# A fused window attention and MLP kernel: the order of the first loads and casts, and the last layer 1 by seven block products

## The chip, the core and the metric

The kernel runs on one core of a Trainium2 chip. The metric is the device time of one execution in microseconds (us), as the median of several executions. Times inside an execution come from the hardware profiler, which records one execution; they are counted from the start of its span. The engines are named as in the profile: PE (TensorE, matrix products), PEld (its weight loads), DVE (VectorE), ACT (ScalarE), POOL (GpSimd) and SP (SyncE, which here only issues loads).

## The reference, cut to what matters

```python
# q, k, v: [8 batches, 8 heads, 576 rows, 64]
scores = (q @ k.T) / 8                       # per batch and head
mask = (rel >= 0) & (rel < 64)               # rel = row of q - row of k
attn = softmax(where(mask, scores, -1e9))
x = (attn @ v), heads side by side           # [8, 576, 512]
xn = (x - mean(x)) / sqrt(var(x) + 1e-6) * g_ln
out = x + relu(xn @ w_ch1) @ w_ch2           # w_ch1 512x2048, w_ch2 2048x512
```
All inputs and the output are fp32; the kernel casts its operands to fp16.

## The kernel before, in words

*Tiles.* Each row sees the 64 rows up to itself, so attention works on blocks of 128 rows: a block needs its own keys and values and the 64 before it. The MLP runs on groups of 512 rows. Groups g = 0 to 7 are the first 512 rows of batch g; the ninth, the tail group (g = 8, `NGRP - 1`, in the code `last`), gathers the last 64 rows of all eight batches. A group has four blocks, called kb or j.

*Attention of one block.* q and k are loaded in halves (`load_qk`, L76), cast to fp16 (`cast_q`, L149) and, for the first three batches, transposed on PE (`t_main`, L268, evicted by `evac`, L262); later batches are transposed by DMA (`x_main`). `load_v` (L161) and `cast_v` (L178) bring v into `vA`; `vB` holds v shifted by 64 rows, made in batch 0 and partly in batch 1 by casts straight from the fp32 load (`vB_cur`, `vB_prev`, L194 and L197). `s_mm` (L302) computes the scores, exponentials on ACT follow, `s_mask` (L355) applies the mask on DVE; in batch 0 PE adds a mask bias instead (`pe_mask`). `b_step` (L369) multiplies by v, divides by the row sum and takes mean and variance; `r_step` (L397) computes the reciprocal deviation on ACT; `z_step` (L406) makes the normalized block z; `zt_step` (L447) transposes z on PE into `zT` and ACT copies it out.

*MLP of one group.* It is a list of small "units", built by `mlp_units` (L503). Layer 1 (`l1`, L508) makes 128 of the 2048 hidden columns for 512 rows in four matmuls of 512 columns, and ACT rectifies the result into `hrT`: 16 such units in groups 2 to 8. Group 0 does half of its layer 1 in halves of 256 rows (`l1_half`, L544), and group 1 all of it. Layer 2 of group 0 is `l2_three` (L557) and `l2` (L521), that of group 1 `l2`. From group 2 on layer 2 is done by `product` (L573): a 2x2 block product with seven block multiplications in place of eight (a Strassen form), each in two units of eight matmuls of 256 columns. It needs sums and differences of blocks of `hrT`, made by `presum` (L493) on DVE as eight additions of 128x1024, and of blocks of w2, made once by `t_weights` (L476). After each product `post` (L600) adds the PSUM bank to the output tile on DVE.

*What sets the order.* The kernel is under a manual schedule: each engine runs its instructions in the order of the program text. In the main loop (L762) every group's units are issued one after the other, and `at(i, f, ...)` hangs a step f behind unit i; so attention of batch g + 1 is interleaved with the MLP of group g by unit numbers written out by hand. `bz` (L769) hangs b_step, r_step and z_step at i, i + 1, i + 2. `pace` (L444) is a tiny POOL copy that makes POOL wait for its operand before the casts behind it.

*The head.* L647 to L654 issue the loads of batch 0 and of w1. w1 comes in eight tiles of 256x512, each cast (and scaled by g) in two parts by `w1_cast` (L232). L666 to L684 hold POOL's casts of batch 0, then memsets for batch 1; L694 to L724 the first scores and blocks, with dummy matmuls (`keep_clock`). Then SP gets batch 1's first half of q and k and the first four w2 loads of 512 KB (L727 to L729). The rest of the loads is issued inside `rest_of_loads` (L731), which hangs at unit 7 of group 0 and also holds POOL's casts in order:

```python
        cast_qk(1, 0)
        for i in range(8):
            w2_cast(i)
            if i < 4:
                w2_load(i + 4)
        load_v(1, 0, 2)
        ...
```
The w2 staging tiles are four buffers (pool `pwst`, tag `wld`), so the load of tile i + 4 comes after the cast of tile i. All loads above are on SP's queue, and their landings are counted by eight semaphores of the program, used in turn.

*The PSUM banks.* Pools `ps_s` (tag `sc`), `ps_x` (`xps`), `ps_t` (`tp`) and `ps_mm` (`mm`) have two buffers of a bank each, `ps_x` one of two banks. Layer 1 takes turns in `mm` and `tp`; `product` holds its X in `tp` and its Y and Z in `mm`. In the tail group no attention is left, so `sc` and `xps` are free.

Of the kernel before, what the change touches and what calls it, by code (L numbers as in the profile page):

```python
# [18 lines left out]
def kernel(  # L19
# [136 lines left out]

    def alloc_v(b):
        vA[b] = p_va.tile([128, 4, H, D + 1], FP16, tag="vA", name=f"vA_{b}")
        nc.gpsimd.memset(vA[b][:, :, :, D:D + 1], 1.0)
# [29 lines left out]
    def init_vB(b):  # L189
        alloc_vB(b)  # L190
        nc.gpsimd.memset(vB[b][:, :, :, D:D + 1], 1.0)
        nc.gpsimd.memset(vB[b][0:64, 0, :, D:D + 1], 0.0)

    def vB_cur(b, c, eng):  # L194
        evac(eng, vB[b][64:128, c, :, 0:D], v32[b][0:64, c])
# [66 lines left out]
    def evac(x, out, in_):  # L262
        if x == 0:
            nc.scalar.copy(out=out, in_=in_)
        else:
            nc.vector.tensor_copy(out=out, in_=in_)
# [235 lines left out]

    def mlp_units(g, split=0, two=False):  # L503
# [123 lines left out]
        if g == 1:  # L627
            return units
        for hc in range(split, NHC):
            units.append(lambda hc=hc: l1(hc))  # L630
# [36 lines left out]
    alloc_qkT(0)  # L667
    cast_q(0, 0, 0)
    alloc_v(0)
    cast_q(0, 1, 0)  # L670
    init_vB(0)
    cast_v(0, 0, 1)
# [3 lines left out]
    cast_v(0, 3, 4)  # L676
    w1_cast(0, 0, nc.gpsimd)
    w1_cast(1, 0, nc.gpsimd, 0, 256)
    w1_cast(1, 0, nc.gpsimd, 256, 512)
    for i, lo in ((2, 0), (3, 0), (2, 256)):  # L680
        w1_cast(i, 0, nc.gpsimd, lo, lo + 256)

    for f in (alloc_qkT, alloc_v, init_vB):
        f(1)  # L684
# [12 lines left out]
    t_main(0, 1, 0, 1)  # L697
    keep_clock(1, ps_mm, "mm")
    vB_cur(0, 0, 0)
    vB_cur(0, 1, 0)  # L700
    vB_prev(0, 0, 1)
    vB_prev(0, 1, 1)
# [13 lines left out]
    vB_cur(0, 3, 1)  # L716
    vB_prev(0, 2, 1)
    keep_clock(1)
    zt_step(0, 1)
    w1_cast(0, 1, nc.scalar)  # L720
# [7 lines left out]
    for i in range(4):  # L728
        w2_load(i)  # L729

    def rest_of_loads():  # L731
        cast_qk(1, 0)
        for i in range(8):
            w2_cast(i)
            if i < 4:
                w2_load(i + 4)
        load_v(1, 0, 2)
        cast_v(1, 0, 1)
        cast_v(1, 1, 2)
        load_qk(1, 1)  # L740
        load_v(1, 2, 4)
        cast_qk(1, 1)
        cast_v(1, 2, 3)
        cast_v(1, 3, 4)
        load_qk(2, 0)
        load_qk(2, 1)
# [15 lines left out]
    for g in range(NGRP):  # L762
# [33 lines left out]
        if g == 0:  # L796
# [29 lines left out]
            at(42, zt_step, 1, 1)  # L826
            at(43, t_main, 1, 0, 1, 0)
            at(44, load_v, 2, 0, 4)
# [10 lines left out]
        if g == 1:  # L839
# [27 lines left out]
            for j in range(4):  # L867
                at((13, 16, 19, 22)[j], s_mm, 2, j)
                at((14, 17, 20, 23)[j], s_mask, 2, j)
                bz((16, 19, 22, 25)[j], 2, j)  # L870
                at((20, 23, 26, 29)[j], zt_step, 2, j)
        if g > 0:
            if g == 1:
                for u, i, c in ((12, 1, 0), (13, 1, 1), (14, 2, 0), (15, 2, 1)):
                    at(u, t_weights, i, c)
            if g == 2:
                at(9, late_masks, 8)
                for u, i, c in ((2, 3, 0), (3, 3, 1), (8, 4, 0), (24, 4, 1)):
                    at(u, t_weights, i, c)
            for u, i, c in () if g == 1 else (  # L880
                    (5, 3, 0), (9, 3, 1), (13, 1, 0), (13, 2, 0), (16, 1, 1), (16, 2, 1), (20, 4, 0), (22, 4, 1)):
                at(u, presum, g, i, c)
# [22 lines left out]
        if 0 < g and b + 1 < B:  # L905
# [5 lines left out]
            if g == 1:  # L911
                at(10, alloc_qkT, n)
                for j, (x, half) in enumerate(((0, 0), (1, 0), (0, 1), (1, 1))):
                    u = (16, 19, 22, 27)[j]
                    at(u, (lambda: pace(zsd[(b, 3)][:, 0:1])) if j == 3 else lambda j=j: pace(rcps[(b, j)][:, 0:1]))
                    at(u, cast_q, n, x, half)
# [61 lines left out]
```

## Time and profile before

| what | value |
|---|---|
| three executions | 303.74, 303.81 and 304.11 us (median 303.81) |
| the profiled execution, as a whole | 304.84 us |
| its span in the profile | 303.0 us |
| mean granted PE clock | 0.993 |
| first scores of the first block start | 10.73 us |
| first use of the fifth w2 tile by PE | 42.82 us |
| layer 1 of the tail group | 271.74 to 285.56 us |
| layer 2 of the tail group | 285.56 to 297.80 us |
| HBM traffic | 36.70 MB read, 9.44 MB written |

A line of the profile's groups reads: source line, engine, operation, tile, count, then busy time, mean of one, and the idle time ahead of them with what ended it. A line of the chain of waits reads: start in us, length in us, engine and tile, source line. A row of the 40 slices shows the busy share in tenths, 7.6 us a digit. In a timeline the first two columns are start and length, and the bracket at the end holds the idle time ahead and what ended it.

### The profile page before, as it was taken

The page shows a single profiled execution, that of the slowest core. Times are in us where ns is not written, and L with a number is a line of the kernel's source. Part 1 is how long each engine was busy: PE and PEld are TensorE (multiplying, and loading weights), DVE is VectorE, ACT ScalarE, POOL GpSimd, SP SyncE. Part 2 cuts the span into 40 slices and gives each one's busy share as a digit, 9 for nine tenths or more (in the row PEclk, how much of TensorE's full clock was granted, in tenths as well). Part 3 has the DMA queues.
Part 4 walks back from the last instruction along what each step waited for, and adds up shares of the span by engine and source line. Part 5 has one row for each costly group of instructions (what it writes and reads, how often), then busy time and mean ns, then how long its engine had stood idle before and what let it go on. Part 6 is the DMA issues. An engine that isn't in the chain of part 4 may idle for free.

```text
span 303.0 us, 7956 instructions
## 1 busy us (share of the span) xinstructions
PE 289.7 (96%) x3259; PEld 187.1 (62%) x3259; DVE 194.8 (64%) x353; ACT 189.9 (63%) x372; POOL 108.8 (36%) x194
## 2 busy tenths in 40 slices
PE   5788999999999999999999999999999999999993
PEld 2456544765854478547855784578457845884582
DVE  0696317457984997389638954895489877641362
ACT  3598733576856894589368937892785978307500
POOL 3778775997786203400440043004171010000000
PEclk9799999999999999999999999999999999999999
DMA  6999799999957969997999899899967930003005
GB/s 186 279 368 386 252 272 276 278 303 279 219 115 209 259 127 168 298 247 128 189 319 228 105 200 322 196 118 204 276 123 153 158 141 0 2 21 117 2 0 138
DMA packets 108371, 58.03 MB, mean 192 GB/s; under 512 B 82240, under 2 KB 98112, under 8 KB 108336
## 3 DMA queue, kind: packets, MB, share of 16 engines
q1 hardware_dynamic: 103696, 45.50, 67.1%
q0 software_dynamic: 3680, 11.52, 12.6%
q10 hardware_dynamic: 960, 0.53, 0.6%
q8 instruction: 25, 0.41, 0.6%
q14 instruction: 10, 0.08, 0.1%
HBM read 36.70 MB, written 9.44 MB: 152 GB/s over the span
## 4 chain that ended last, share of the span: by engine, by line
PE 75%; DMA 11%; SPq 5%; POOL 3%; ACT 2%; DVE 2%; issue 1%; POOLq 0%
PE hps L512 33%; PE wX L590 16%; PE wZ L590 8%; PE wY L590 4%; DMA v<-in_v_dram 4%; PE xps L383 4%; SPq L83 3%; DMA w2s<-in_moe_w_ch_dram 3%; PE sc L326 2%; PE ch L525 2%; DMA vt<-vA 2%; SPq L173 2%; PE hph L549 2%; DMA qk<-in_k_dram 1%; PE ztp L453 1%; PE sc L333 1%
## 5 line engine op out<-in xcount | busy, mean ns | idle before, releaser
L512 PE MATMUL hps<-zT,w1g 128*128 128x512 f16 x480 | 109.7, 379 | 0.0
L516 ACT ACTIVATE hrT<-hps 128x512 f16<-128x512 f32 x120 | 71.3, 596 | 54.0 <-PE hps L512 52.8
L512 PEld LDWEIGHTS <-w1g 128*128 128x128 f16 x480 | 44.8, 98 | 49.5
L590 PEld LDWEIGHTS <-sw 128*128 128x128 f16 x448 | 43.5, 98 | 5.0
L590 PEld LDWEIGHTS <-hrT 128*128 128x128 f16 x336 | 32.4, 98 | 5.4
L367 DVE TENSOR_TENSOR pt<-pt,mask 128x1024 f16<-128x1024 f16 x28 | 20.0, 713 | 20.9 <-ACT pt L347 12.6
L207 POOL DMA_DIRECT2D vB<-vA x10 | 5.1, 518 | 77.9 <-ACT vA L145 77.6
L472 POOL DMA_DIRECT2D out_dram<-osb x20 | 13.2, 660 | 54.4 <-DVE osb L608 50.1
L392 DVE BATCH_NORM_STATS2 stats<-xn 128x6 f32<-128x512 f32 x36 | 25.0, 695 | 1.2
L390 DVE TENSOR_TENSOR xn<-xps,rcp 128x512 f32<-128x512 f32 x36 | 24.9, 691 | 1.2
L347 ACT ACTIVATE pt<-sc 128x512 f16<-128x512 f32 x40 | 23.7, 594 | 2.5 <-PE sc L326 2.5
L501 DVE TENSOR_TENSOR sw<-hrT 128x1024 f16<-128x1024 f16 x28 | 19.0, 678 | 9.7 <-ACT hrT L516 9.7
L549 PE MATMUL hph<-zT,w1g 128*128 128x256 f16 x192 | 23.7, 273 | 0.4 <-POOL w1g L240 0.2
L414 DVE TENSOR_SCALAR z<-xn,mv,rs 128x512 f16<-128x512 f32 x32 | 19.8, 617 | 5.0 <-ACT rs L404 4.5
L608 DVE TENSOR_TENSOR osb<-wX,xn 128x512 f32<-128x512 f32 (+1 forms) x24 | 14.9, 621 | 9.9 <-PE wX L590 9.9
L353 ACT ACTIVATE pt<-sc 128x512 f16<-128x512 f32 x32 | 17.6, 594 | 5.0 <-PE sc L333 4.6
L147 POOL CAST qk<-qk 128x1024 f16<-128x1024 f32 x16 | 17.1, 1076 | 9.0 <-DMA qk<-in_q_dram 6.0
L549 PEld LDWEIGHTS <-w1g 128*128 128x128 f16 x192 | 17.9, 98 | 3.5 <-POOL w1g L240 0.5
L383 PEld LDWEIGHTS <-pt 128*64 128x64 f16 x576 | 12.1, 110 | 12.8 <-issue 8.5
L525 PE MATMUL ch<-w2s,hrT 128*128 128x512 f16 x80 | 19.8, 379 | 0.0
L456 ACT COPY zT<-ztp 128x512 f16<-128x512 f16 x21 | 12.3, 584 | 9.6 <-PE ztp L453 9.5
L554 ACT ACTIVATE hrT<-hph 128x512 f16<-128x512 f32 x24 | 14.2, 598 | 3.4 <-PE hph L549 3.2
(108 smaller groups left out, 439.3 us busy)
## 6 DMA issues: line engine op xcount, KB each, us to landing
w2s<-in_moe_w_ch_dram SPq DMA_DIRECT2D x12, 512.0 KB, 9.4
out_dram<-osb POOLq DMA_DIRECT2D x12, 512.0 KB, 7.0
qk<-in_q_dram SPq DMA_DIRECT2D x10, 512.0 KB, 7.7
qk<-in_k_dram SPq DMA_DIRECT2D x10, 512.0 KB, 9.5
v<-in_v_dram SPq DMA_DIRECT2D x40, 128.0 KB, 5.9
qk<-in_q_dram SPq DMA_DIRECT2D x12, 256.0 KB, 5.0
qk<-in_k_dram SPq DMA_DIRECT2D x12, 256.0 KB, 4.8
v<-in_v_dram SPq DMA_DIRECT2D x12, 256.0 KB, 5.7
```

Source lines behind the costliest of these rows:

```text
L347: nc.scalar.activation(out=pt[:, par].rearrange("k h w (p j) -> k (h w) p j", j=4), in_=sc[:, :].rearrange("k h w (j p) -> k (h w) p j", j=4),
L367: nc.vector.tensor_tensor(out=ptv, in0=ptv, in1=mb, op=ALU.mult)
L383: nc.tensor.matmul(out=xps[64 * r:64 * r + 64, h, :D + 1], lhsT=pt[:, par, hp, r, :], rhs=rhs, start=True, stop=True)
L390: nc.vector.tensor_tensor(out=xn, in0=xps[:, :, 0:D], in1=rcp_b, op=ALU.mult)
L392: nc.vector.bn_stats(out=stats, in_=xn.rearrange("p h d -> p (h d)"))
L414: nc.vector.tensor_scalar(out=z, in0=x, scalar1=mv[:, 0:1], scalar2=rss[(g, kb)][:, 0:1], op0=ALU.subtract, op1=ALU.mult)
L501: nc.vector.tensor_tensor(out=S[i], in0=a, in1=b, op=op)
L512: nc.tensor.matmul(out=hps, lhsT=w1g[:, kc, 128 * hc:128 * (hc + 1)], rhs=zT[g][:, kc, :], start=(kc == KCS[0]), stop=(kc == KCS[-1]),)
L516: nc.scalar.activation(out=hrT[:, hc, :], in_=hps, func=AF.Relu, bias=0.0, scale=1.0)
L525: nc.tensor.matmul(out=ch[kb], lhsT=hrT[:, hc, 128 * kb:128 * (kb + 1)], rhs=w2s[:, hc, :], start=(hc == 0), stop=(hc == NHC - 1),)
L549: nc.tensor.matmul(out=hps[:, e], lhsT=w1g[:, kc, 128 * hc:128 * (hc + 1)], rhs=zT[g][:, kc, 256 * half:256 * half + 256], start=(kc == KC ...
L590: nc.tensor.matmul(out=xyz[bank][t * two_banks][:, t], lhsT=lhsT, rhs=rhs, start=bool(first and (t == 0 or two_banks) and hc == 0), stop=( ...
```

## The change

1. *First casts.* The cast of the first half of k of batch 0 goes from POOL to DVE, in two instructions (`cast_k0`), and the eviction of its transposition from DVE to ACT. Of the vB casts of batch 0, those of blocks 0 and 1 all go to DVE, two of the later ones to POOL (a new case `x == 2` in `evac`). Two w1 casts go to DVE. The memsets of batch 1 (`alloc_qkT`, `alloc_v`, `init_vB`) move ahead of the first casts on POOL.
2. *Loads of batch 1.* v and the second half of q and k of batch 1 are issued behind the first four w2 loads, ahead of w2 loads five to eight. In `rest_of_loads` their casts move between the w2 casts, and the loads of q and k of batch 2 forward to the places of the casts.
3. *Slots in group 0.* `t_main(1, 0, 1, 0)` comes before `zt_step(1, 1)`; the load of v of batch 2 is issued four units earlier.
4. *Slots in group 1.* Some b_step, zt_step and cast slots of batch 2 and 3 move one unit later.
5. *The tail group's layer 1.* It is done by seven block multiplications in place of eight: `l1_seven` has 28 units of four matmuls of 256 columns in place of 16 units of four matmuls of 512. Sums of w1 blocks (`l1_wsum`, eight DVE instructions of 128x1024) and of zT blocks (`l1_zsum`, four of 128x512) are made in group 7, in buffers of the q and k loads. Results of n = 2, 5, 6 are copied by ACT into held tiles, that of n = 4 is rectified by ACT, those of n = 1, 7, 3 are added to a held one and then rectified, two DVE instructions each. The presums of layer 2 hang at later units of the tail group, and its first product is inserted among the last units of layer 1.

```diff
+    def cast_k0():
+        t = qk32.pop((0, 1, 0))
...
+        for e in range(2):
+            nc.vector.tensor_copy(out=dst[:, :, e], in_=t[:, 512 * e:512 * e + 512].rearrange("p (j d) -> p j d", d=D))
...
+        elif x == 2:
+            nc.gpsimd.tensor_copy(out=out, in_=in_)
...
+    def l1_wsum(i, c):
+        A = [[w1g[:, 2 * kb + c, 1024 * d:1024 * d + 1024] for kb in range(2)] for d in range(2)]
+        if c == 0:
+            s1w[i] = p_in.tile([128, 2, 1024], FP16, tag=f"qk32_{i % 2}", name=f"s1w_{i}")
...
+        nc.vector.tensor_tensor(out=S[i], in0=a, in1=b, op=op)
...
+    def l1_zsum(g, i):
+        if i % 2:
+            s1z[i // 2] = p_in.tile([128, 2, 2, 256], FP16, tag=f"qk16_{i // 2}", name=f"s1z_{i}")
...
+        nc.vector.tensor_tensor(out=T[i], in0=z_block(g, *a), in1=b, op=ALU.subtract)
...
+    def l1_seven(g, hrT):
...
+        def product(r, n):
...
+                    nc.tensor.matmul(out=ps[:, e], lhsT=lhsT, rhs=rhs, start=bool(first and e == 0 and c == 0),
+                                     stop=(e == 1 and c == 1), skip_group_check=True)
...
+            if n in (2, 5, 6):
+                held[(r, n)] = p_pt.tile([128, 2, 256], FP32, tag="pt", name=f"l1h_{r}_{n}")
+                nc.scalar.copy(out=held[(r, n)], in_=ps)
+            elif n == 4:
+                nc.scalar.activation(out=hrT[:, down, lo], in_=ps, func=AF.Relu, bias=0.0, scale=1.0)
+            else:
+                out, other = {1: (hrT[:, up, lo], 2), 7: (hrT[:, down, hi], 5), 3: (hrT[:, up, hi], 6)}[n]
+                nc.vector.tensor_tensor(out=out, in0=ps, in1=held.pop((r, other)), op=ALU.add)
+                nc.vector.tensor_scalar(out=out, in0=out, scalar1=0.0, scalar2=None, op0=ALU.max)
...
+        if last:
+            units += l1_seven(g, hrT)
+            units.insert(24, lambda: product(1, 0))
+            units.append(lambda: product(1, 1))
+            for n in (2, 6, 5, 7, 3, 4):
+                for t in range(2):
+                    units.append(lambda n=n, t=t: product(n, t))
+            return units
...
     alloc_qkT(0)
+    alloc_qkT(1)
+    alloc_v(0)
+    alloc_v(1)
     cast_q(0, 0, 0)
-    alloc_v(0)
-    cast_q(0, 1, 0)
     init_vB(0)
+    init_vB(1)
+    cast_k0()
...
+    vB_prev(0, 2, 2)
+    vB_cur(0, 3, 2)
     w1_cast(0, 0, nc.gpsimd)
-    w1_cast(1, 0, nc.gpsimd, 0, 256)
-    w1_cast(1, 0, nc.gpsimd, 256, 512)
...
-    t_main(0, 1, 0, 1)
+    t_main(0, 1, 0, 0)
     keep_clock(1, ps_mm, "mm")
-    vB_cur(0, 0, 0)
-    vB_cur(0, 1, 0)
+    vB_cur(0, 0, 1)
     vB_prev(0, 0, 1)
+    vB_cur(0, 1, 1)
     vB_prev(0, 1, 1)
...
-    vB_cur(0, 3, 1)
-    vB_prev(0, 2, 1)
+    w1_cast(0, 1, nc.vector)
     keep_clock(1)
     zt_step(0, 1)
-    w1_cast(0, 1, nc.scalar)
+    w1_cast(1, 0, nc.vector)
...
     for i in range(4):
         w2_load(i)
+    load_v(1, 0, 2)
+    load_qk(1, 1)
+    load_v(1, 2, 4)
...
             if i < 4:
                 w2_load(i + 4)
-        load_v(1, 0, 2)
-        cast_v(1, 0, 1)
-        cast_v(1, 1, 2)
-        load_qk(1, 1)
-        load_v(1, 2, 4)
-        cast_qk(1, 1)
+            if i == 3:
+                load_qk(2, 0)
+                cast_v(1, 0, 1)
+                cast_v(1, 1, 2)
+            if i == 5:
+                cast_qk(1, 1)
+                load_qk(2, 1)
         cast_v(1, 2, 3)
         cast_v(1, 3, 4)
-        load_qk(2, 0)
-        load_qk(2, 1)
...
-            at(42, zt_step, 1, 1)
-            at(43, t_main, 1, 0, 1, 0)
-            at(44, load_v, 2, 0, 4)
+            at(42, t_main, 1, 0, 1, 0)
+            at(43, zt_step, 1, 1)
+            at(40, load_v, 2, 0, 4)
...
-                bz((16, 19, 22, 25)[j], 2, j)
-                at((20, 23, 26, 29)[j], zt_step, 2, j)
+                bz((16, 20, 23, 25)[j], 2, j)
+                at((20, 24, 27, 29)[j], zt_step, 2, j)
...
+            if g == NGRP - 2:
+                for u, i, c in ((14, 3, 0), (15, 3, 1), (17, 1, 0), (18, 1, 1), (20, 2, 0), (22, 2, 1),
+                                (24, 4, 0), (26, 4, 1)):
+                    at(u, l1_wsum, i, c)
+                for u, i in ((24, 1), (26, 2), (28, 3), (28, 4)):
+                    at(u, l1_zsum, g + 1, i)
             for u, i, c in () if g == 1 else (
+                    (23, 1, 0), (24, 2, 0), (28, 1, 1), (28, 2, 1), (29, 3, 0), (30, 3, 1), (31, 4, 0), (32, 4, 1)
+                    ) if g == NGRP - 1 else (
...
-                    u = (16, 19, 22, 27)[j]
+                    u = (16, 20, 23, 27)[j]
```

## The prediction

> **What bounds the kernel now.** I read the page first (busy shares, the 40 slices), then the chain that ended last, then the timelines of the SP queue, POOL and PE over 20 to 56 us, then PE and DVE over the last 45 us.
>
> ```profile
> PE 289.7 (96%) x3259; PEld 187.1 (62%) x3259; DVE 194.8 (64%) x353; ACT 189.9 (63%) x372; POOL 108.8 (36%) x194
> ...
> PE   5788999999999999999999999999999999999993
> ```
> PE is the bound: no other engine passes 64%, and the PE row is short of full only in the first three slices (7.6 us each) and the last. Each pause of PE after about 26 us therefore moves the end by its own length, unless PE was going to pause there anyway. There are few: 0.49 us at 53.7 us, and about 0.3 and 0.2 us at 71 and 79 us.
>
> ```profile
> 271.74 13.81 PE hps L512 x64
> 285.56 1.75 PE wX L590 x16
> ...
> 296.04 1.76 PE wX L590 x16
> 297.80 0.02 issue
> 297.82 0.42 DVE osb L608
> ```
> The end of the chain: PE runs the tail group without a gap, then one DVE addition and the last store. 64 matmuls of 512 columns take 13.81 us, 216 ns each; 16 of 256 columns take 1.75 us, 109 ns each.
>
> ```profile
> 23.73 15.00 SPq L245 DMA_DIRECT2D w2s<-in_moe_w_ch_dram  x8
> 38.79 1.18 SPq L173 DMA_DIRECT2D v<-in_v_dram  x2
> 40.01 4.71 SPq L83 DMA_DIRECT2D qk<-in_q_dram  x2
> 44.77 2.43 SPq L83 DMA_DIRECT2D qk<-in_k_dram  x2
> 47.24 1.22 SPq L173 DMA_DIRECT2D v<-in_v_dram  x2
> ```
> SP issues all eight w2 loads (23.73 to 38.73) before v and the second half of q and k of batch 1. This is the order that the change turns round.
>
> ```profile
> 27.79 9.39 DMA w2s<-in_moe_w_ch_dram
> 37.30 1.05 POOL w2s L250
> ```
> The fourth w2 load lands 9.39 us after its issue, at 37.18: it stands in a queue.
>
> ```profile
> 33.27 1.04 POOL L250 CAST w2s<-w2s 128x1024 f16<-128x1024 f32 x1 [0.33 <-DMA w2s<-in_moe_w_ch_dram]
> ...
> 35.93 1.04 POOL L250 CAST w2s<-w2s 128x1024 f16<-128x1024 f32 x1 [0.29 <-DMA w2s<-in_moe_w_ch_dram]
> 37.30 1.04 POOL L250 CAST w2s<-w2s 128x1024 f16<-128x1024 f32 x1 [0.33 <-DMA w2s<-in_moe_w_ch_dram]
> 38.63 1.04 POOL L250 CAST w2s<-w2s 128x1024 f16<-128x1024 f32 x1 [0.29 <-DMA w2s<-in_moe_w_ch_dram]
> ...
> 44.36 1.04 POOL L250 CAST w2s<-w2s 128x1024 f16<-128x1024 f32 x1 [0.46 <-DMA w2s<-in_moe_w_ch_dram]
> ```
> Column one is the start, the bracket the idle time before it. Each cast starts when its load lands, 1.34 us apart: 512 KB per 1.34 us is what the queue delivers. The eighth ends at 45.40.
>
> ```profile
> 41.09 5.79 PE L563 MATMUL ch<-w2s,hrT 128*128 128x512 f16 x26
> ```
> When PE needs them: 10 matmuls of this product lie before 41.09, the fifth w2 tile (i = 4) is first used by the 19th, at 41.09 + 8 x 0.216 = 42.82; the next by the 25th (44.12), the 31st (45.41) and the 37th (47.18, after one attention step). Their casts ended at 39.67, 42.16, 43.90 and 45.40. The slack is 3.2, 2.0, 1.5 and 1.8 us.
>
> [...] SP's loads land in the order of issue, so a load put in front delays all behind it. [...] the DMA share falls to 0.38 in 34 to 36 us, though the third and fourth w2 loads are open until 35.8 and 37.18[...]. [...] 216 and 109 ns; the trace has both, so halving the width loses only 1%. [...]
>
> **1. First casts.** The k cast of the first half goes from POOL (1.04 us from 7.46) to DVE in two pieces, the second of which can run as its load lands at 7.34 (0.43 us by the 64x512 cast row), its eviction from DVE (1.23) to ACT (1.01), and the v casts from ACT to DVE and from DVE to POOL. First scores come about 0.6 us earlier. The second half's casts start as its loads land (10.92, 12.83), unmoved, so no more than 0.6 is passed on there; DVE takes two w1 casts (0.5 to 0.9 each) before the third block and may give some back. I bound it at -1.3 to +0.3 on PE's arrival at layer 1. The memsets that move forward lie in POOL's idle stretch before 4.79. Worth to the end: nothing, if step 2 makes PE wait later.
>
> **2. Loads of batch 1.** v and the second half of q and k (eight loads of 256 KB) now stand on SP before the fifth w2 load. In the program each SP load waits for the landing of the one eight before it; so the fifth w2 load, issued at 34.34 before, now comes after the fourth has landed (37.18), and behind 2 MB. Per load, q or k takes 0.67 us (half of 1.34) and v 1.03 (the casts of v on ACT that start as it lands are at 45.39 and 46.42). Landing of the fifth w2: 37.18 + 4 x 1.03 + 4 x 0.67 + 1.34 = 45.3; then 46.7, 48.0, 49.3. POOL casts the fifth and sixth by 46.5 and 47.8; the new order puts the two q/k casts next (2 x 1.04, to 49.9), so the seventh ends at 51.05 and the eighth at 52.1. PE waits at 42.82 until 46.5 (+3.7), runs on at 216 ns, and waits again at its 31st matmul until 51.05, against 45.41: **+5.65 us**. The eighth is then in time (needed at 52.7). Behind the waiting matmul stands all of PE's program. The long pause may halve the clock ([...]PEclk shows 0.5 after the pause at 7 us), but the half-speed stretch would lie before 51.05 and cost nothing.
> Lower end: [...]the unused DMA time of 34 to 44 us (0.67 x 2 us plus about 0.15 x 8 us, near 2.7 us) absorbs as much: the fifth lands near 42.4, the seventh cast ends at 48.1: +2.7. Upper end: w2 loads five to eight took up to 2 us apart in 38 to 44 us; at that rate +7.7. I take 5.65.
> What is late next: v of batch 1 (landed 45.37, cast 46.29, needed 46.80) gets ample slack. The batch 2 loads come later by at most 2 us while PE is 5.65 later.
>
> **3. Swap at the end of group 0.** The batch 1 transposition moves ahead of the second zT step, which now directly precedes its user. The 0.49 us wait goes (1.3 us of PE work comes before it), but PE then waits for transposition, ACT copy (0.59) and hand-over: layer 1 starts at 55.55 instead of 55.26, +0.3.
>
> **4. Later steps in group 1.** One unit more of room before two steps: removes most of 0.3 + 0.2: -0.5 (bounds -0.5 to +0.2).
>
> **5. Group 7.** DVE gets eight 128x1024 additions (0.68) and four 128x512[...]: 7 us in 257 to 272 us, where it works 60%. Each result addition has 1.0 us before PE wants its bank. Placed in order, the tightest starts at 265.35 and ends 266.0, due 266.5. No wait; cover 0.5 us. ACT is idle there.
>
> **6. Tail layer 1.** 112 matmuls of 256 columns instead of 64 of 512: 112 x 0.1094 = 12.25 against 13.81: -1.56. But 12 of 28 results now need a DVE addition (0.69) and a rectification[...]. From the third on, DVE runs without a gap; the presums for layer 2 end near 288.8 where product 6 wants them at 287.9: +0.9, and +0.1 at the next bank. Net **-0.55** (bounds -1.3 to +0.3).
>
> **Sum.** 5.65 + 0.3 - 0.5 - 0.55 = +4.9 on the profiled span of 303.0: 307.9. That execution took 304.84 as a whole, 1.03 above the median of 303.81; the difference goes on the median: **308.7**.
>
> **Rivals.**
> (a) *Half hidden*: the bandwidth spare at 34 to 44 us takes half of it, step 2 costs 2.7: 303.81 + 2.7 - 0.75 = 305.8. For it: the share of 0.38; against: landings stayed 1.34 us apart right through it.
> (b) *Faster*: the w2 loads land in time, because 2 MB fit into the spare DMA time. Then the head's 0.7, step 4 and the tail count: 303.81 - 0.7 + 0.3 - 0.5 - 0.55 = 302.3. It decides at a fifth w2 cast ending before 42.8 and a seventh before 45.4. For it: slices of 252 to 276 GB/s there against 386 before; against: the issue itself is after 37.18, and a w2 load takes 4.2 us from issue to landing even with little before it (34.34 to 38.51).
> (c) *Slower still*: w2 at 2 us each, +7.7: 310.8.
>
> **Chances.** Forecast 58% (its own range 307.2 to 310), (a) 22%, (b) 15%, (c) 5%. The range from 304.6 to 311.0 leaves out (b) and part of (c). About 0.2% is what a measurement of this kernel can tell. Slower 0.82, same 0.04 (the upper edge of b, the lower of a), faster 0.14.
>
> **What would show it.** PE's ch matmuls in group 0 waiting on POOL w2s, some 3.7 and 2 us, near 42 and 49 us; the fifth w2 cast starting near 45.4 and the seventh near 50; the first scores 0.6 us earlier than 10.73, with no worth; in the tail PE from the first block product to the last matmul in 25.5 us instead of 26.06, with a wait on DVE sw near 0.9 us. If the ch matmuls show no wait on POOL, step 2 is wrong and (b) holds.

## The result, and the profile after

The changed kernel takes 313.98 us (median of 4 executions, 312.69 to 314.26) against 303.77 us before: ratio 1.0326, 95% interval 1.0296 to 1.0356. It is slower by 10.2 us; the forecast was 308.7, the upper end of its range 311.0. The profiled execution took 313.80 us, its span is 312.1 (before: 304.84 and 303.0). In what follows a median is over all executions of a kernel, while a ratio and its interval (95%) leave out the executions that took over 1.5% more than the kernel's fastest.

The page of the changed kernel (busy shares, then PE and its granted clock in 40 slices):

```profile
PE 290.2 (93%) x3307; PEld 191.8 (61%) x3307; DVE 211.8 (68%) x392; ACT 188.3 (60%) x370; POOL 106.8 (34%) x193
...
PE   5778949899999999999999999999999999999983
...
PEclk9999997999999999999999999999999999999998
```
PE's busy time is nearly the same (289.7 before), because two terms cancel: the tail's matmuls take 1.56 us less, and some matmuls in group 0, as shown below, take 1.5 us more. So 8.6 of the 9.1 us of longer span are idle time of PE. The hole is in slice 6 (39 to 47 us), where PE stood at 9 before, and the clock dips in slice 7, right behind it. DVE rose from 194.8 to 211.8 us.

PE's timeline in the changed kernel:

```profile
40.86 1.90 PE L649 MATMUL ch<-w2s,hrT 128*128 128x512 f16 x8
47.34 5.74 PE L649 MATMUL ch<-w2s,hrT 128*128 128x512 f16 x18 [4.58 <-POOL w2s L257]
...
60.83 0.61 PE L281 MATMUL tp<-ident,qk 128*128 128x128 f16 x8 [1.39 <-ACT zT L465]
...
63.20 2.78 PE L635 MATMUL hph<-zT,w1g 128*128 128x256 f16 x24 [0.67 <-ACT zT L465]
```
The wait for the fifth w2 tile is where the forecast put it, ahead of the 19th matmul of this product (before: 42.82 without a wait). The 18 matmuls behind it take 5.74 us, though 18 x 0.216 is 3.9. Then come two waits at the end of group 0; the kernel before had one there, 0.49 us at another step. (A bracket counts from the end that the profile gives the matmul before. In the text below, a wait of PE is the distance between two starts less the usual distance, which is some 0.16 us more: 4.75 for the 4.58 here.)

SP's queue and POOL's timeline in the changed kernel:

```profile
23.69 4.42 SPq L252 DMA_DIRECT2D w2s<-in_moe_w_ch_dram  x4
28.36 4.16 SPq L180 DMA_DIRECT2D v<-in_v_dram  x2
32.56 4.16 SPq L83 DMA_DIRECT2D qk<-in_q_dram  x2
36.77 1.25 SPq L83 DMA_DIRECT2D qk<-in_k_dram  x2
38.06 1.56 SPq L180 DMA_DIRECT2D v<-in_v_dram  x2
39.72 4.93 SPq L252 DMA_DIRECT2D w2s<-in_moe_w_ch_dram  x4
```
```profile
46.25 1.04 POOL L257 CAST w2s<-w2s 128x1024 f16<-128x1024 f32 x1 [7.21 <-DMA w2s<-in_moe_w_ch_dram]
47.58 1.04 POOL L257 CAST w2s<-w2s 128x1024 f16<-128x1024 f32 x1 [0.29 <-DMA w2s<-in_moe_w_ch_dram]
48.56 2.03 POOL L147 CAST qk<-qk 128x1024 f16<-128x1024 f32 x2
50.53 2.03 POOL L257 CAST w2s<-w2s 128x1024 f16<-128x1024 f32 x2
```
The fifth w2 load is issued at 39.72 and landed at 46.13 (forecast 45.3); POOL stands idle 7.21 us for it. It landed 9.82 us after the fourth, where the forecast had 8.14: the four loads of v took 4.13 us together and the two of q 0.67 each, as priced, but the two of k 1.33 and 1.51 in place of 0.67, and the w2 load itself 1.51 in place of 1.34. The seventh cast ends at 51.57 (forecast 51.05).

PE, DVE, ACT and POOL by stretches (PEclk is the last column but two, 1.00 is full speed):

```profile
48.00:49.00 1.00, 1.00 (x3) 0.29 (x2) 0.00 (x0) 0.00 (x0) 1.00 (x2) 0.50 1.00 381
50.00:51.00 1.00, 1.00 (x5) 0.35 (x4) 0.00 (x0) 0.00 (x0) 1.00 (x2) 0.78 1.07 404
52.00:53.00 1.00, 1.00 (x6) 0.29 (x3) 0.00 (x0) 0.00 (x0) 1.00 (x2) 1.00 1.04 381
```
After the pause PE runs at half clock until about 50.4: these matmuls start 0.427 us apart, not 0.216.

The end of the chain of waits in the changed kernel:

```profile
282.83 0.59 ACT l1h L576
...
283.47 0.60 PE l1Z L571 x4
...
289.28 0.61 DVE hrT L581
...
289.93 0.61 PE l1Z L571 x4
...
296.86 0.70 DVE sw L510
297.58 0.70 DVE sw L510
...
298.33 1.48 PE wX L676 x12
...
306.89 0.42 DVE osb L694
```
In the tail the chain is no longer PE's alone: it crosses ACT once and lies on DVE for most of 285 to 298 us. PE's three waits there, in its timeline:

```profile
283.47 0.60 PE L571 MATMUL l1Z<-s1z,s1w 128*128 128x256 f16 x4 [0.24 <-ACT l1h L576]
...
289.93 0.60 PE L571 MATMUL l1Z<-zT,s1w 128*128 128x256 f16 x4 [0.19 <-DVE hrT L581]
...
298.33 1.48 PE L676 MATMUL wX<-tw,sw 128*128 128x256 f16 x12 [0.82 <-DVE sw L510]
```
From start to start they are 0.40, 0.35 and 0.97 us.

**Where the time goes, step by step.** I cut PE's timeline at five starts: the first matmul of group 0's layer 1 with 512 columns ("arrival", 30.21 us before), the first b_step of batch 1 (46.80), group 1's layer 1 (55.27), group 2's layer 1 (92.42), the tail group (271.58); and at the last addition on DVE (297.82). The differences from the kernel before, in us:

| kernel | arrival | w2 loads | end of group 0 | group 1 | groups 2 to 7 | tail |
|---|---|---|---|---|---|---|
| changed kernel | -0.23 | +6.44 | +1.72 | +0.94 | 0.00 | +0.21 |
| p1_head | -0.65 | 0.00 | -0.14 | -0.28 | 0.00 | 0.00 |
| p2_loads | -1.02 | +8.93 | +0.13 | +0.06 | 0.00 | 0.00 |
| p3_swap | -1.25 | 0.00 | +1.05 | -0.24 | +2.60 | 0.00 |
| p4_slots | -1.07 | 0.00 | +0.09 | +0.82 | 0.00 | 0.00 |
| p5_tail | -0.01 | 0.00 | -0.06 | +0.74 | 0.00 | +0.22 |
| m1_w2first | -1.02 | +8.37 | +1.45 | +0.94 | 0.00 | +0.22 |
| m2_six | -1.38 | +7.33 | -0.25 | -0.28 | 0.00 | 0.00 |
| m5_latecast | -1.02 | +8.17 | +0.28 | +1.11 | 0.00 | +0.21 |
| m6_keepclock | -1.32 | +5.46 | +0.72 | +0.59 | 0.00 | +0.21 |
| m8_slots26 | -1.45 | 0.00 | +0.05 | +0.20 | +0.55 | 0.00 |

The first row adds up to 9.08, the growth of the span. Two readings of the table come ahead of all others. The arrival differs by up to 1.9 us between executions even where nothing ahead of it was changed (28.35 to 30.21 in 13 profiles of kernels with the first casts of before, middle 29.14), and the profile of before is the latest of them. (Left out are m12_lateact and m13_order, whose profiled executions took 741.78 and 307.23 us.) And a column is the same to 0.01 us where PE never waits in it, so a difference there is a wait that can be looked up. It need not come from the edit: the 2.60 of p3_swap is two waits for a DMA (1.77 and 0.57 us) ahead of score matmuls in later groups, and its median doesn't show them; m8_slots26 has one of that kind (0.36).

### The profile page after: what moved, and what is told of

Read it like the earlier page. It is cut to its first block, busy times and chain, and to the rows that moved or that the text cites. A ratio compares the mean times of both kernels' runs of the same rounds, so it can differ in the third digit from the quotient of the medians.

```text
span 312.1 us, 8114 instructions
## 1 busy us (share of the span) xinstructions
PE 290.2 (93%) x3307; PEld 191.8 (61%) x3307; DVE 211.8 (68%) x392; ACT 188.3 (60%) x370; POOL 106.8 (34%) x193
## 4 chain that ended last, share of the span: by engine, by line
PE 68%; DMA 9%; DVE 9%; SPq 8%; POOL 2%; issue 2%; ACT 1%; DVEq 0%; POOLq 0%
PE hps L598 27%; PE wX L676 15%; PE wZ L676 8%; SPq L83 4%; PE wY L676 4%; PE xps L392 3%; DMA qk<-in_q_dram 3%; PE sc L335 2%; SPq L180 2%; DVE hrT L581 2%; DMA w1s<-in_moe_w_ch_dram 2%; DMA w2s<-in_moe_w_ch_dram 2%; DMA v<-in_v_dram 2%; PE ch L611 2%; PE ch L649 2%
## 5 line engine op out<-in xcount | busy, mean ns | idle before, releaser
L598 PE MATMUL hps<-zT,w1g 128*128 128x512 f16 x416 | 95.7, 380 | 0.0
L602 ACT ACTIVATE hrT<-hps 128x512 f16<-128x512 f32 x104 | 61.7, 596 | 39.6 <-PE hps L598 38.4
L598 PEld LDWEIGHTS <-w1g 128*128 128x128 f16 x416 | 38.6, 98 | 42.1
L412 ACT ACTIVATE rs<-mv,epst 128x1 f32<-128x1 f32 x36 | 10.8, 299 | 20.8 <-DVE mv L403 20.7
L396 DVE RECIPROCAL rcp<-xps 128x8 f32<-128x8 f32 x36 | 7.3, 202 | 23.2 <-PE xps L392 23.2
L635 PEld LDWEIGHTS <-w1g 128*128 128x128 f16 x192 | 18.1, 98 | 5.4 <-POOL w1g L247 1.3
L147 POOL CAST qk<-qk 128x1024 f16<-128x1024 f32 x15 | 15.5, 1041 | 7.0 <-PE tp L281 2.9
```

The lines of the kernel that those rows point to most:

```text
L598: nc.tensor.matmul(out=hps, lhsT=w1g[:, kc, 128 * hc:128 * (hc + 1)], rhs=zT[g][:, kc, :], start=(kc == KCS[0]), stop=(kc == KCS[-1]),)
L602: nc.scalar.activation(out=hrT[:, hc, :], in_=hps, func=AF.Relu, bias=0.0, scale=1.0)
L635: nc.tensor.matmul(out=hps[:, e], lhsT=w1g[:, kc, 128 * hc:128 * (hc + 1)], rhs=zT[g][:, kc, 256 * half:256 * half + 256], start=(kc == KC ...
```

## The experiments

The theory after the traces: four terms of the forecast were off, each for a reason of its own. The rival to it is that one thing, the late loads, drags all the others along. So the parts were first put on the kernel before one at a time. Medians of before on the chips used lie between 303.65 and 304.37.

**p1_head.** Part 1 of the change alone.
```diff
-    cast_q(0, 1, 0)
+    cast_k0()
...
```


> The kernel before with part 1 alone (first casts, evictions, memsets). Trace theory: the scores come 0.8 us earlier as in the changed kernel, but the later casts wait for loads, and PE gets to the layer 1 of group 0 only some 0.2 us earlier: 303.6 us. Prediction's bounds: -1.3 to +0.3, so 302.5 to 304.1. A rival, that DVE's new casts delay the third block: slower than 304.1.


304.05 us, ratio 0.999 (0.9965 to 1.0014): no difference. The first scores come at 9.51 us (10.73 before), and PE arrives at layer 1 at 29.56, within the spread of kernels with the old casts. What is won ahead is lost at the w1 tiles: at the first matmul of layer 1 PE is still 1.04 us earlier than before (18.83 and 19.87), then it waits (1.03 in the bracket) for a w1 cast on DVE, which starts when its load has landed (19.57), and eight matmuls later 0.09 of the lead is left.

**p2_loads.** Part 2 alone.
```diff
+    load_v(1, 0, 2)
+    load_qk(1, 1)
+    load_v(1, 2, 4)
...
```


> The kernel before with part 2 alone (order of batch 1 loads and their casts). Prediction: the seventh w2 cast ends at 51.05, 5.65 us late: 309.4 us. Trace theory: the seventh cast ends at 51.6 as in the changed kernel (+6.2), and z of the first block of batch 1 on DVE collides with two POOL casts (1.2 us more, which reach PE through the second zT step): 311.0 to 311.3. If the loss of the changed kernel comes from another part, 304 to 306.


312.41 us, ratio 1.025 (1.0215 to 1.0285): most of the loss, and more than either number. The fifth w2 load landed at 46.94, PE waited from 41.80 to 48.16, and about 12 matmuls behind it ran at 0.427 us. The second half of what I expected failed: z of block (1, 0) took 1.10 us and not some 2, and the end of group 0 stands at +0.13.

**p3_swap.** Part 3 alone.
```diff
-            at(42, zt_step, 1, 1)
-            at(43, t_main, 1, 0, 1, 0)
+            at(42, t_main, 1, 0, 1, 0)
+            at(43, zt_step, 1, 1)
...
```


> The kernel before with part 3 alone (transposition ahead of the second zT step, v of batch 2 four units earlier). Prediction: +0.3, 304.1 us. Trace theory: the swap by itself costs 0.5 (the transposition takes the bank that the first zT copy must leave), and the other 1.2 us seen at this place in the changed kernel came from a slow z on DVE, which is absent here: 304.3. Rival, that the swap makes all of it: 305.5.


304.27 us, ratio 1.0016 (0.9987 to 1.0045). In the trace +1.05 at the end of group 0. z of block (1, 0) took 1.31 us on DVE there (0.77 before): 0.54 of it is that, 0.5 is the swap. In the trace the wait for the second z ahead of its transposition (0.49 in the bracket) is gone, and in its place PE waits ahead of the batch 1 transposition, by the profile for ACT's copy of the first zT, and ahead of layer 1 for ACT's copy of the second zT (0.67 in the bracket).

**p4_slots and m8_slots26.** Part 4 alone; then with the fourth b_step one unit later still, and with it its zT step and the last cast and transposition of batch 3.
```diff
-                bz((16, 19, 22, 25)[j], 2, j)
+                bz((16, 20, 23, 25)[j], 2, j)      # p4_slots
+                bz((16, 20, 23, 26)[j], 2, j)      # m8_slots26
```


> The kernel before with part 4 alone (slots in group 1). Prediction: -0.5, 303.3 us. Trace theory: b_step of the third block moves to unit 23 and that of the fourth stays at 25, so DVE has two units in place of three between them, and the fourth b_step waits for its mask: +0.9, 304.7. Rival: the waits at this place of the changed kernel came from the later loads, and the slots alone change nothing: 303.8.

> As the kernel with part 4 alone, with the fourth b_step of batch 2 one unit later too (26), so that three units lie between it and the third as before. If the shorter distance is what costs 0.8 us (DVE needs 2.4 us from the third b_step to the mask of the fourth): the step in group 1 goes from +0.8 to between -0.3 and 0.1, 303.6 us. If a later place as such costs: +0.8 or more, 304.6.


p4_slots: 305.01 us, ratio 1.0036 (1.0011 to 1.0061), +0.82 in group 1. m8_slots26: 304.37, ratio 1.0002 (0.9978 to 1.0026), +0.20. PE and DVE of p4_slots around the fourth b_step:

```profile
86.25 0.22 PE L383 MATMUL xps<-vB,pt 128*64 128x65 f16 x1 [0.55 <-DVE pt L367]
```
```profile
83.76 0.19 DVE L387 RECIPROCAL rcp<-xps 128x8 f32<-128x8 f32 x1
...
85.53 0.66 DVE L367 TENSOR_TENSOR pt<-pt,mask 128x1024 f16<-128x1024 f16 x1
```
From the third b_step on DVE needs 2.4 us (rcp, xn, statistics, then the mask of the fourth block); with two units between the two b_steps PE is there 0.55 us earlier. With three units the wait is gone. What is left of the step, 0.2, is a wait of 0.26 at 78 us, which p4_slots has too (0.32). These two waits are the evidence, and not the size of the column: in kernels with the old slots it runs from -0.28 to +0.74, because a wait for the second block's mask comes and goes there (1.0 in p5_tail, where the mask takes 1.48 us on DVE in place of 0.66). The intervals of the two ratios overlap.

**m1_w2first, m6_keepclock, m2_six.** Is it the cast order, the clock or the bytes? m1 is the changed kernel with the q/k casts behind all w2 casts; m6 adds dummy matmuls in the pause; m2 is the kernel before with six of the eight loads moved.
```diff
-            if i == 5:
-                cast_qk(1, 1)
-                load_qk(2, 1)
+        cast_qk(1, 1)
+        load_qk(2, 1)
...
             at(7, rest_of_loads)
+            at(24, keep_clock, 22)                 # m6_keepclock only
```
```diff
         w2_load(i)
+    load_v(1, 0, 2)                                # m2_six
+    load_qk(1, 1)
...
-        load_v(1, 0, 2)
         cast_v(1, 0, 1)
         cast_v(1, 1, 2)
-        load_qk(1, 1)
```


> The changed kernel with POOL's two q/k casts of batch 1 put behind all w2 casts. The prediction's reading (PE at full speed waits for the seventh w2 cast, which stands behind those two casts): the seventh cast ends near 49.9 in place of 51.6, and 1.5 us are won: 312.4 us. The trace's reading: after its pause PE runs its next eight matmuls at half clock and reaches the 31st matmul only at 51.45, so the cast order is worth no more than 0.2 us: 313.8. It may also move the collision of z with POOL's casts, by up to 1.2 us either way.

> As m1_w2first, with 22 dummy matmuls (22 x 0.216 = 4.75 us) ahead of the 19th matmul of layer 2 in group 0, so that PE is busy while it would wait for the fifth w2 cast. If the half clock after the pause is what costs m1_w2first its last 2.3 to 2.8 us: the 18 matmuls after the pause take 18 x 0.216 = 3.9 us in place of 6.7, and the first b_step of batch 1 starts near 51.5 in place of 54.15; about 311.5 us against 314. If PE waits for casts there in any case: no change, 314.

> The kernel before with six of the eight loads of batch 1 (v of the first two blocks, the second half of q and k) ahead of the fifth w2 load, and the casts in the order of before. If the bytes ahead of the w2 loads set their landing: the fifth lands near 44.2 in place of 46.1 to 46.9 and its cast ends at 45.3, so PE waits some 2.5 to 3.3 us, and with one window of half clock behind it the loss is 2.5 to 4.8: 306.3 to 308.6. If not the bytes but the place in the order of issue counts, the loss is as with all eight: 311 to 312.


m1: 314.81 us, ratio 1.0314 (1.0229 to 1.0399); m6: 311.2, 1.0285 (1.0217 to 1.0353); m2: 310.23, 1.0213 (1.0175 to 1.0251). The executions of m1 (310.91 to 318.12) and m6 (310.4 to 314.54) overlap, so what the dummies do is read in the traces. PE's timeline in m1_w2first, then in m6_keepclock:

```profile
40.06 1.90 PE L649 MATMUL ch<-w2s,hrT 128*128 128x512 f16 x8
47.46 6.75 PE L649 MATMUL ch<-w2s,hrT 128*128 128x512 f16 x18 [5.50 <-POOL w2s L257]
```
```profile
41.50 4.91 PE L785 MATMUL warm<-mbias,ident 128*128 128x512 f16 x22
46.25 2.77 PE L649 MATMUL ch<-w2s,hrT 128*128 128x512 f16 x12
49.56 1.46 PE L649 MATMUL ch<-w2s,hrT 128*128 128x512 f16 x6 [0.54 <-POOL w2s L257]
```
The same stretch by PEclk, m1_w2first ahead of m6_keepclock:

```profile
48.00:49.00 1.00, 1.00 (x4) 0.30 (x2) 0.00 (x0) 0.00 (x0) 0.75 (x1) 0.50 1.00 379
```
```profile
48.00:49.00 1.00, 1.00 (x5) 0.38 (x4) 0.00 (x0) 0.00 (x0) 0.53 (x1) 1.00 1.06 408
```
In m1 all casts are in time, and yet the 18 matmuls take 6.75 us. With the dummies the first 12 take 2.6 (12 x 0.216) and the only wait left is a short one for the seventh cast; the column "w2 loads" falls from 8.37 to 5.46. Of these 2.91 us the clock makes 2.0: its term of 2.72 goes and a wait of 0.70 for the seventh cast comes; the other 0.91 is a shorter pause (4.75 in place of 5.66), since the fifth cast ended earlier in this execution. The clock is a term of its own. It closes the account in each kernel: wait for the fifth tile plus 0.211 (0.427 - 0.216) for every matmul at half clock, with parts of one where the clock changes inside it.

| kernel | wait for the fifth tile | matmuls at half clock | sum | column |
|---|---|---|---|---|
| changed kernel | 4.75 | 7.2 = 1.51 (+0.18 for the seventh cast) | 6.44 | 6.44 |
| p2_loads | 6.36 | 12.2 = 2.58 | 8.94 | 8.93 |
| m1_w2first | 5.66 | 12.9 = 2.72 | 8.38 | 8.37 |
| m5_latecast | 5.22 | 14 = 2.95 | 8.17 | 8.17 |
| m2_six | 4.72 | 12.4 = 2.62 | 7.34 | 7.33 |

Not all of the clock's term is a loss: PE at full clock would have waited for the seventh cast in its place, until 51.6 in the changed kernel (nothing is lost there), 52.4 in p2_loads and 51.7 in m5_latecast (0.9 lost in each). In m1_w2first, whose seventh cast ends at 50.07, the 2.7 are lost in full.

m2 leaves open how much the bytes count. With two loads fewer ahead the fifth cast starts 8.98 us after the fourth; with all eight it is 9.37 (m6_keepclock), 9.8 to 9.9 (three kernels) and 10.97 (p2_loads). That is 0.4 to 2.0 us less, where two loads of v were priced at 2.1. I had expected a landing at 44.2 and a loss of 2.5 to 4.8. The fifth cast started at 45.06 and the trace lost 7.3, since PE came 1.4 us early and the clock stayed at half for as long as with eight (12.4 matmuls, 12.2 in p2_loads). The median lies nearer to the branch in which the place in the order of issue counts (311 to 312) than to that of the bytes (306.3 to 308.6). Which of the two it is, isn't shown.

**m5_latecast.** The changed kernel, with POOL's next casts held until the second z is there.
```diff
-            at(28, cast_q, 2, 0, 0)
-            at(29, cast_q, 2, 1, 0)
-            at(29, make_vB_half, 1)
...
+            at(39, lambda: pace(zsd[(1, 1)][:, 0:1]))
+            at(39, cast_q, 2, 0, 0)
+            at(39, cast_q, 2, 1, 0)
+            at(39, make_vB_half, 1)
```


> The changed kernel with POOL's first two casts of q and k of batch 2 and its copies for vB of batch 1 held until the second z of batch 1 is there. If z of the first block took 1.98 us on DVE because POOL's casts ran beside it: z takes 0.55 to 0.6, and the way from the first b_step of batch 1 to layer 1 of group 1 becomes about 1.2 us shorter (9.0 in place of 10.2 us). If the swap of the two PE steps makes all of the 1.7: no change there.


313.25 us, ratio 1.0312 (1.0277 to 1.0348); the end of group 0 goes from +1.72 to +0.28. DVE and POOL of the changed kernel, then DVE of m5_latecast:

```profile
55.97 1.98 DVE L423 TENSOR_SCALAR z<-xn,mv,rs 128x512 f16<-128x512 f32 x1
...
60.34 0.55 DVE L423 TENSOR_SCALAR z<-xn,mv,rs 128x512 f16<-128x512 f32 x1
```
```profile
55.64 2.03 POOL L147 CAST qk<-qk 128x1024 f16<-128x1024 f32 x2
```
```profile
56.91 0.55 DVE L423 TENSOR_SCALAR z<-xn,mv,rs 128x512 f16<-128x512 f32 x1
...
59.84 0.55 DVE L423 TENSOR_SCALAR z<-xn,mv,rs 128x512 f16<-128x512 f32 x1
```
z ends 0.29 us after POOL's second cast (57.95 and 57.66): two casts in a row lie beside it, and it takes 1.98 us. In the kernel before one cast lies beside it (POOL 49.21 to 50.25, z 49.76 to 50.53): z takes 0.77 us and ends 0.28 us after the cast. With the casts held back it takes 0.55 (m5_latecast, both blocks). So z on DVE took longer beside POOL's casts and ended just after them in both profiles; by what mechanism is not shown. From z the delay goes on through the statistics of block (1, 1) (57.87 to 59.74 in the changed kernel) to the reciprocal deviation on ACT (59.77 to 60.30), behind which the zT copy is queued (60.21 to 60.78), and so to the transposition on PE (60.83). The numbers add: 0.5 for the swap plus the growth of z over 0.77 gives 1.71 (changed kernel, 1.72), 1.04 (p3_swap, 1.05) and 0.28 (m5_latecast, 0.28). Two kernels that played no part in finding the 0.5 fit too: m1_w2first (z 1.70: 1.43, measured 1.45) and m6_keepclock (z 0.99: 0.72, measured 0.72).

**p5_tail, m9_norect.** Part 5 alone; then without the twelve separate rectifications.
```diff
-                nc.vector.tensor_scalar(out=out, in0=out, scalar1=0.0, scalar2=None, op0=ALU.max)
```


> The kernel before with part 5 alone (layer 1 of the tail group by seven products). Prediction: -0.55, 303.25 us. Trace theory: PE saves 1.56 us of matmuls and waits 0.40 us for ACT's copies, 0.35 for DVE's rectification and 0.97 for the sums of the sixth product: +0.2, 304.0.

> As the kernel with part 5 alone, but without the rectification of the results of n = 1, 7 and 3 in the tail group's layer 1: three quarters of its hidden values stay unrectified. It takes 12 x 0.2 to 0.3 us off DVE and puts it nowhere. If DVE's load is the cause, the waits of 0.35 and 0.97 us go and that of 0.40 on ACT stays: tail step near -1.1 in place of +0.22, 302.6 us. If single places set the waits: -0.1 to +0.2, 303.9.


p5_tail: 304.61 us, ratio 1.0013 (0.9994 to 1.0032), tail +0.22, to 0.01 as in the changed kernel. (Its +0.74 in group 1 is one wait of 1.0 for a mask on DVE, which the changed kernel hasn't.) m9_norect: 302.94, ratio 0.9969 (0.9949 to 0.9989), tail -1.19: of the three waits only that on ACT is left. So the two that end on DVE, 0.35 and 0.97, need DVE's load.

**m4_tailpool, m3_tailrelu, m10_fiveact, m7_fivefirst.** Four ways to relieve DVE or go round it: the twelve rectifications on POOL, on ACT, the last five on ACT, and the fifth product ahead of the sixth.
```diff
-                nc.vector.tensor_scalar(...)
+                nc.gpsimd.tensor_scalar(...)                    # m4_tailpool
+                nc.scalar.activation(..., func=AF.Relu, ...)    # m3_tailrelu; five of twelve: m10_fiveact
...
-            for n in (2, 6, 5, 7, 3, 4):
+            for n in (2, 5, 6, 7, 3, 4):                        # m7_fivefirst
```


> As the kernel with part 5 alone, with the twelve separate rectifications on POOL in place of DVE. If DVE's load in the tail is what turns the gain into a loss: DVE has 12 x 0.29 = 3.5 us less to do, the waits on DVE go (0.35 and 0.97), the wait on ACT (0.40) stays: 303.8 - 1.56 + 0.4 = 302.7 us. If POOL's work on the same tiles is slow or holds DVE up: 304 or more.

> As the kernel with part 5 alone, with the twelve separate rectifications on ACT. ACT then has 28 instructions of about 0.5 us in the 14 us of this stretch, so it may be the next bound: if it keeps up, 302.7 us; if its queue is late instead of DVE's, 303.5 to 304.3.

> As the kernel with part 5 alone, with the last five of the twelve rectifications on ACT, after ACT has made its last copy of a held result. DVE loses 5 x 0.2 to 0.29 = 1.0 to 1.4 us ahead of the sums for the sixth product, whose wait of 0.97 should go to 0 to 0.2; 0.40 and 0.35 stay: tail step -0.6 to -0.8, 303.1 us. If ACT is held up by waiting for DVE's additions as in m3_tailrelu: +0.2 or more.

> As the kernel with part 5 alone, with the fifth product of the tail's layer 2 ahead of the sixth. It needs the first sum only, which is ready 0.7 us before the second. If the 0.97 us of wait is the second sum being late on DVE: about 0.2 to 0.3 us of it is left, the tail step goes from +0.22 to about -0.5, and 303.3 us. If DVE is late by its whole queue, the wait only moves to the next product: 304.0.


None is better than p5_tail: 310.39 us (1.0211, 1.0167 to 1.0256; tail +6.54), 308.56 (1.0164, 1.0112 to 1.0216; +4.09), 305.78 (1.0046, 1.0023 to 1.0069; +0.33) and 305.42 (1.0063, 1.004 to 1.0085; +1.34). One line of each, POOL of m4_tailpool, then PE of m3_tailrelu, m10_fiveact and m7_fivefirst:

```profile
275.58 15.04 POOL L573 TENSOR_SCALAR hrT<-hrT 128x512 f16<-128x512 f16 x10 [0.74 <-DVE hrT L572]
```
```profile
275.00 0.60 PE L562 MATMUL l1Z<-s1z,s1w 128*128 128x256 f16 x4 [2.27 <-ACT l1h L567]
```
```profile
285.15 0.82 PE L670 MATMUL wY<-w2s,hrT 128*128 128x256 f16 x6 [0.64 <-ACT hrT L569]
```
```profile
293.36 1.91 PE L667 MATMUL wX<-w2s,sw 128*128 128x256 f16 x16 [1.76 <-DVE osb L685]
```
POOL takes 1.50 us for what DVE does in 0.29. On ACT rectifications wait for DVE's additions (0.54 to 1.47 us at a time in m3_tailrelu), and what PE needs is queued behind them: the copies of held results in m3, the last n = 4 results in m10. In m10 the 0.97 is gone, as expected, but new waits of 0.80 and 0.36 for those n = 4 results come ahead of it, and the 0.40 and 0.35 stay; its interval overlaps that of p5_tail. In m7 the wait only moves one product on, to a bank that DVE hasn't emptied yet (1.76 in the bracket).

**m11_best.** m10_fiveact with the held casts of m5_latecast.
```diff
+                if (r, n) in ((1, 3), (2, 7), (3, 7), (2, 3), (3, 3)):
+                    nc.scalar.activation(out=out, in_=out, func=AF.Relu, bias=0.0, scale=1.0)
+                else:
                     nc.vector.tensor_scalar(out=out, in0=out, scalar1=0.0, scalar2=None, op0=ALU.max)
...
+            at(39, lambda: pace(zsd[(1, 1)][:, 0:1]))
...
```


> As m10_fiveact, with POOL's first casts of batch 2 and its copies for vB held until the second z of batch 1 is there (as in m5_latecast), loads, slots and first casts as before. z of batch 1 then never runs beside POOL's casts of batch 2; before, it lost 0.2 us there: 302.9 us. If the casts of batch 2 then come late for their transpositions in group 1: over 304.


304.8 us, ratio 1.0023 (1.0004 to 1.0041): no gain; the tail stands at +0.33 and the end of group 0 at 0.00: the first z took 0.55 us as expected, but the second 0.97.

**m12_lateact, m13_order.** As m10_fiveact, with the last two rectifications behind ACT's other results; m13 also exchanges two pairs of blocks. In both, the second halves of the first and second sum read the last two n = 3 results before they are rectified.
```diff
+                if (r, n) in ((2, 3), (3, 3)):
+                    late_l1.append(lambda: nc.scalar.activation(out=out, in_=out, func=AF.Relu, bias=0.0, scale=1.0))
...
+                    at(28, lambda: [f() for f in late_l1])
...
-(0, 6), (1, 5), (1, 6), (2, 2), (0, 7)
+(0, 6), (2, 2), (1, 5), (1, 6), (0, 7)
...
-(3, 6), (1, 3), (2, 7), (1, 4), (3, 7)
+(3, 6), (2, 7), (1, 3), (1, 4), (3, 7)
```


> As the kernel with part 5 alone, with five rectifications on ACT, of which the two of the last n = 3 results come behind ACT's last result of n = 4 (in m10_fiveact they stood ahead of it and held up the second product by 0.83 us). Nothing on ACT then waits ahead of something that PE wants soon, and DVE has 1.0 to 1.4 us less to do: the wait of 0.97 goes, 0.40 and 0.35 stay: tail step -0.8, 303.1 us. If DVE is still late: -0.3 to +0.2.

> As m12_lateact, with two blocks of the tail's layer 1 exchanged with their neighbours, so that the second n = 5 and the second n = 3 result don't follow at once on the first ones, with which they share a PSUM tile. If the waits of 0.40 and 0.35 us come from that tile: tail step -1.2 to -1.5, 302.5 us, faster than before. If they come from ACT and DVE being late: -0.8 as in m12_lateact.


m12: 304.59 us, ratio 1.0008 (0.9983 to 1.0032); its profiled execution took 741.78 us, so its tail isn't read. m13: 303.11, ratio 0.9947 (0.9925 to 0.9969), tail -1.35, and PE waits for no longer than 0.2 us from the first block product to the last matmul. (Its profiled execution took 307.23 us; what is too long in it lies ahead of the tail, at the arrival, the end of group 0 and in groups 2 to 7.) The second n = 5 and the second n = 3 result in m13_order:

```profile
278.40 0.60 PE L562 MATMUL l1Z<-s1z,s1w 128*128 128x256 f16 x4
...
284.75 0.60 PE L562 MATMUL l1Z<-zT,s1w 128*128 128x256 f16 x4
```
m10_fiveact, with the same rectifications on ACT up to there and the old order, has both waits (0.40 and 0.36). So the 0.40 and 0.35 us go with the order of blocks that share a tile, though they end on ACT and DVE; the 0.35 goes with a lighter load of DVE too (m9_norect). A kernel that does all of the work would have 2 x 0.21 = 0.42 us more on DVE (0.21 from the start of a rectification to that of the next instruction, 283.90 and 284.11 in m7_fivefirst) ahead of those sums, which come just in time here (they end at 291.35, the half that they feed is read from 291.74); by that, as an estimate, a tail step of about -1.3 is possible. It wasn't tried.

## Why the prediction was wrong, step by step

The forecast was +4.9 us, the medians differ by 10.2. No single step makes the 5.3 us between them: step 3 makes 1.4, step 4 1.4, the way to the median 1.1, steps 2 and 6 0.8 each, and 0.2 come off at PE's arrival.

*Step 1 (casts)*: right. The scores come 0.9 us earlier, and no gain is left at the matmuls of layer 1 with 512 columns (p1_head).

*Step 2 (loads)*: the mechanism was right, with the place, the two tiles and the order of waits, and it is most of the loss. The term was mis-sized: 5.65 forecast, 6.44 in the profile. The seventh cast ends at 51.57, not 51.05 (0.52), and PE came 0.23 earlier to the same wait. Behind the 0.52 stands the price of the loads: the two of k took 1.33 and 1.51 us, 0.67 each in the forecast. In p2_loads (8.93) and m5_latecast (8.17) the seventh cast ends at 52.40 and 51.62 (1.35 and 0.57), PE came 1.02 earlier in both, and the half clock adds 0.9: 8.9 and 8.1. So the sentence "the half-speed stretch would lie before 51.05 and cost nothing" held in the changed kernel's profile, where the stretch is short, and failed in the others. From PE's restart the clock stays at half for 3.0 us in the changed kernel and for 5.3 to 6.1 us in four others (p2_loads, m1_w2first, m2_six, m5_latecast). By PEclk the half clock sets in just ahead of the restart in the changed kernel and lasts from 47.0 to 50.4 us, 3.4 us; in p2_loads and m1_w2first it lasts about 6.8 us (46.6 to 53.4 and 46.1 to 53.0, estimated from the mean clock of the stretches). Why it lasts twice as long there is not shown. The lower end of the forecast has a slip: spare DMA time of 2.7 us would leave 5.65 - 2.7 = 2.95 us, and 2.7 us stands there. That the spare time would be used was the author's estimate; the fifth load landed at 46.13, not near 42.4.

*The way to the median*: the forecast put the difference on a median 1.03 us below the profiled time. Here that is not allowed. The profile of before was late at PE's arrival, 30.21 against 29.14 in the middle of the others; but the end of the wait for w2 is set by landings, so an execution whose PE comes 1 us earlier waits 1 us longer. What the median was better by is lost in the changed kernel. m5_latecast, whose edit changes nothing ahead of that step, shows it: its PE came 0.79 us earlier than in the changed kernel, and its first b_step started 0.94 later. With arrivals counted from 29.14 the changed kernel's row of the table comes to 10.15 us and that of m5_latecast to 9.82; their medians are 10.21 and 9.60 above those of before. So this is about 1.1 us of the miss; it is worked out from the arrivals, not tried by itself.

*Step 3 (swap)*: +0.3 forecast, +1.72 measured. What failed is the list of what else changes there: with the loads of step 2 POOL's casts of batch 2 fall beside z, +1.2, and the swap itself costs 0.5, because the batch 1 transposition waits too (for ACT's copy of the first zT), which the forecast left out. The +0.28 of m5_latecast is 0.5 less 0.22 for a z that runs faster than before, so that it comes near the forecast is chance.

*Step 4 (slots)*: the sign was wrong, -0.5 forecast, +0.8 (p4_slots) and +0.94 (changed kernel) measured. I read two waits that would go and not the distance to the fourth b_step, which shrank from three units to two.

*Step 5 (sums in group 7)*: right, groups 2 to 7 stand at 0.00. In the changed kernel a sum of w1 blocks (128x1024) took 0.68 us and one of zT blocks (128x512) 0.42.

*Step 6 (tail)*: the saving of 1.56 and the wait at the sixth product (0.9 forecast, 0.97 measured) were right. What a rectification takes was the author's estimate, no trace had shown it; in the changed kernel it took 0.29 us, and the addition ahead of it 0.68. Missing were the waits of 0.40 and 0.35 for the shared tile of n = 5 and n = 3: -1.56 + 0.40 + 0.35 + 0.97 = +0.16, measured +0.21.

The rival of one common cause fell: parts 4 and 5 cost alone what they cost together, and by medians the five parts alone come to -0.1, +8.2, +0.1, +0.8 and +0.7 us, 9.7 in sum against 10.2 for the whole. Only z took longer in the whole (1.98 us) than in part 2 (1.10) or part 3 (1.31) alone. Of the forecast's rivals, (a) and (b) fell with the first wait on w2; (c) was nearest, though the w2 loads landed 1.34 us apart and not 2.

## What to carry to other kernels

Here eight loads moved ahead in SP's queue cost the bound engine the later landing (the fifth w2 load at 46.13 us in the changed kernel, 38.51 before) and, where the pause of PE was 4.7 to 6.4 us, also the half clock behind it (7.2 to 14 matmuls at 0.427 us in place of 0.216); and since landings then set the time, what PE was early by was lost too (about 1.1 us). Before loads are moved ahead elsewhere, count what lands later. When matmuls are traded for additions elsewhere, add up that engine's load over the whole stage and look for tiles that two results share, before counting the saved matmuls. Moving a step by a unit changes two distances; check the one behind it.

## What the runs showed of the hardware beyond that

A rectification of 128x512 fp16 in SBUF took 0.29 us on DVE (changed kernel), 0.62 on ACT (m3_tailrelu) and 1.50 on POOL (m4_tailpool). PE's first matmul of layer 1 with 512 columns came anywhere between 28.35 and 30.21 us in 13 profiles with the same program ahead of it, so a difference of less than 1.9 us between two single profiles of the head is no evidence.
